# Attention with a relative-position bias and a mixture of adapters: two stages through DRAM rewritten as one hand-ordered pass over head pairs

## The chip, the cores and the metric

The kernel runs on one core of a Trainium2 chip. The metric is device time in microseconds (us) of one execution. A run is called slow when it is over 1.5% above the fastest of the same kernel. Engines: PE multiplies matrices and writes the results to a memory called PSUM (copying them out is called an eviction), ACT is ScalarE (exponentials and copies), DVE is VectorE (elementwise work), POOL is GpSimd (here it mostly issues loads that cast), SP issues other transfers.

## The reference, cut to what matters

There are 8 batches, 8 heads, 576 tokens and head dimension 64, all in float32. The attention has no mask. Its bias depends only on the distance of two tokens, through a table of 32 buckets per head; the last bucket holds for every distance of 128 or more.

```python
scores = q @ k.T / 8                      # per batch and head, 576 x 576
bias   = bias_table[bucket(|i - j|)]      # a Toeplitz matrix per head
x      = softmax(scores + bias) @ v       # -> 4608 tokens x 512
# experts: 8 adapters of rank 16; each token uses the two with the largest x @ w_gate
out    = x + sum over 2 experts of w_e * (x @ A[e]) @ B[e]
```

## The kernel before

It has two stages with DRAM between them, scheduled by a framework. Stage one goes head by head. Scores are held transposed (keys on partitions), so that the product with the values needs no transpose, and the bias is applied as a factor `exp(bias)` after the exponential:

```python
for jb in range(JB):                       # 5 blocks of keys (4 x 128 + 64)
    for n0, n1 in ((0, 512), (512, S)):
        nc.tensor.matmul(sc[:P, n0:n1], lhsT=kTs[:, jb*128:jb*128+P],   # 64 rows: one head
                         rhs=qTs[:, n0:n1], start=True, stop=True)
    nc.scalar.activation(e[:P, :], sc[:P, :], ACT.Exp, scale=scale)
    nc.vector.tensor_tensor(p[:P, :], e[:P, :], ebias[(h, jb)][:P, :], op=ALU.mult)
    for n0, n1 in ((0, 512), (512, S)):
        nc.tensor.matmul(pv[:, n0:n1], lhsT=v1[:P, jb, :],              # 64 + 1 columns
                         rhs=p[:P, n0:n1], start=(jb == 0), stop=(jb == JB - 1))
nc.vector.tensor_copy(o, pv[:D, :])         # then to DRAM as xT_d
nc.vector.tensor_copy(rsb, pv[D:D + 1, :])  # row sums, to DRAM as well
```

Ahead of it q, k and v are cast through DRAM to bf16, and 40 tiles `ebias` of 576 columns are built. Stage two reads x and the reciprocal sums back in 36 tiles of 128 tokens, and for each tile runs the gate (about ten small VectorE operations), the two expert matmuls, and four matmuls with an identity that add the residual.

The softmax here doesn't subtract the row's maximum and nothing guards it: scores larger than these inputs give would overflow.

## Time and profile before

The median was 625.53 us of three runs (622.73 to 628.53). These three lines are from the page of the kernel before: PE's busy time, then PE's busy share and its granted clock in 40 slices of the span, in tenths.

```profile
PE 453.0 (73%) x1960; PEld 181.3 (29%) x1960; DVE 326.4 (53%) x949; ACT 283.9 (46%) x537; POOL 193.1 (31%) x431
...
PE   0000895768899999999999999999999404555554
...
PEclk9999999999655555555555555555555556565556
```

The next lines are stretches of the span (from:to in us, length, then busy us and instruction count of PE, PE's weight loads, DVE, ACT and POOL, then the granted clock, as a share of full speed, the DMA share and GB/s).

```profile
core 0: us, PE busy (x) PEld busy (x) DVE busy (x) ACT busy (x) POOL busy (x), PEclk, DMA share, GB/s
62.00:150.00 88.00, 66.33 (x263) 24.73 (x264) 35.67 (x71) 53.62 (x89) 18.68 (x38) 1.00 0.77 189
200.00:450.00 250.00, 243.58 (x979) 91.25 (x978) 146.44 (x294) 134.37 (x216) 79.13 (x162) 0.50 0.36 79
520.00:600.00 80.00, 45.02 (x283) 26.70 (x282) 67.03 (x367) 31.35 (x115) 34.23 (x56) 0.56 0.89 234
```

From 200 to 450 us PE is busy for 243.58 of 250 us, at half clock, and no other engine comes near that: this stretch is bound by PE. After 520 us DVE leads.

The costliest groups of instructions (line, engine, operation, names, shapes, count | busy us, mean ns | idle time before them and what ended it). For a matmul, `64*128 64x512` says that the trace gives 64 active rows and 128 active columns for the weights, and 512 columns of the other operand; a "column" below is one of these 512, and "rows" are the 64.

```profile
L176 ACT ACTIVATE e<-sc 128x576 bf16<-128x576 f32 x256 | 161.8, 648 | 154.2 <-PE sc L171 116.9 <-PE pv L182 17.0 <-DVE p L179 9.8
L171 PE MATMUL sc<-pTq,pTk 64*128 64x512 bf16 x256 | 148.6, 595 | 15.4 <-ACT e L176 14.1 <-ACT pTk L149 0.7
L179 DVE TENSOR_TENSOR p<-e,ebias 128x576 bf16<-128x576 bf16 x256 | 105.2, 444 | 116.7 <-ACT e L176 98.7 <-ACT ebias L96 17.8
L171 PE MATMUL sc<-pTq,pTk 64*128 64x64 bf16 x256 | 63.2, 247 | 0.0
```

Two lines of PE's timeline (start us, us from the first start to the last end) show what the clock does. Both are 8 matmuls of the values, 4 x (512 + 64) columns:

```profile
145.78 2.13 PE L182 MATMUL pv<-p,v_914 128*65 128x512 bf16 x8
...
150.21 1.18 PE L182 MATMUL pv<-p,v_970 128*65 128x512 bf16 x8
```

The first took 2.13 us, the second 1.18. The clock record has only the values 0.5 and 1, and the second line lies in one of its few full stretches. **A trap:** the record begins at its first change, and the profile counts everything earlier as full. The 9s of the first ten slices are mostly wrong: until about 149 us the pace is that of half clock. Mean clocks of whole runs suffer from this too: 0.639 is listed for this trace, and 0.52 is left when the first 149.2 us are counted as half.

### The profile page before, as it was taken

The numbers are of one execution on the slowest core, as the hardware profiler recorded it, in microseconds if no ns is written. First come the engines' busy times: TensorE is split into PE (matmuls) and PEld (weight loads), VectorE is DVE, ScalarE is ACT, GpSimd is POOL, SyncE is SP. The second block draws the span as 40 slices with busy tenths as digits, with TensorE's granted clock in tenths as the row PEclk, the third lists the DMA queues.
The fourth block names the chain that finished last, engine by engine and source line by source line (L and its number), as shares of the span: only waits on it lengthen the run. The fifth ranks groups of instructions, "written<-read, shape, count | busy, mean of one in ns | idle before, by whom it ended". The sixth has DMA issues, their size and how long they took to land. (4 is left out here: it accounts for less than half of the span.)

```text
span 620.8 us, 7660 instructions
## 1 busy us (share of the span) xinstructions
PE 453.0 (73%) x1960; PEld 181.3 (29%) x1960; DVE 326.4 (53%) x949; ACT 283.9 (46%) x537; POOL 193.1 (31%) x431
## 2 busy tenths in 40 slices
PE   0000895768899999999999999999999404555554
PEld 0000331223333333333333333333333102333332
DVE  0000453237555656656565655656566417888884
ACT  0021674557554545555455555555555203333333
POOL 7040123114342423433232322323231055344420
PEclk9999999999655555555555555555555556565556
DMA  5999589669876775942222232101010089989872
GB/s 114 227 248 243 130 247 215 155 160 225 184 164 123 191 144 167 199 122 58 49 48 40 44 58 44 29 20 31 19 29 20 21 137 214 234 217 245 234 190 103
DMA packets 134388, 82.96 MB, mean 134 GB/s; under 512 B 110144, under 2 KB 115520, under 8 KB 134344
## 3 DMA queue, kind: packets, MB, share of 16 engines
q1 hardware_dynamic: 116168, 49.26, 31.2%
q0 software_dynamic: 13056, 28.48, 23.1%
q10 hardware_dynamic: 5120, 4.72, 2.4%
q8 instruction: 16, 0.26, 0.2%
q14 instruction: 28, 0.23, 0.1%
HBM read 67.93 MB, written 28.64 MB: 156 GB/s over the span
## 5 line engine op out<-in xcount | busy, mean ns | idle before, releaser
L176 ACT ACTIVATE e<-sc 128x576 bf16<-128x576 f32 (+1 forms) x320 | 201.0, 647 | 167.3 <-PE sc L171 126.1
L171 PE MATMUL sc<-pTq,pTk 64*128 64x512 bf16 (+3 forms) x640 | 209.9, 424 | 15.7 <-ACT e L176 14.3
L179 DVE TENSOR_TENSOR p<-e,ebias 128x576 bf16<-128x576 bf16 (+1 forms) x320 | 133.2, 445 | 142.5 <-ACT e L176 116.1
L171 PEld LDWEIGHTS <-pTk 64*128 64x128 bf16 (+1 forms) x640 | 56.5, 118 | 136.6 <-issue 132.8
L188 DVE CAST o<-pv 64x576 bf16<-64x576 f32 x64 | 48.0, 749 | 71.3 <-PE sc L171 58.3
L238 POOL DMA_DIRECT2D dv<-recips_d x72 | 44.1, 617 | 57.2 <-DVE lm L258 15.5
L143 PE MATMUL tpk<-ident,ntk 128*128 128x128 bf16 (+1 forms) x160 | 29.1, 284 | 38.9 <-DMA ntk<-k_bf 38.8
L96 ACT ACTIVATE ebias<-eb_tmp 128x576 bf16<-128x576 f32 (+1 forms) x40 | 26.7, 680 | 62.7 <-DMA eb_tmp<-gext_d 62.7
L192 DVE COPY rsb<-pv 1x576 f32<-1x576 f32 x64 | 48.1, 752 | 2.0
L143 PE MATMUL tpq<-ident,ntq 128*128 128x128 bf16 (+1 forms) x160 | 26.6, 287 | 24.2 <-DMA ntq<-q_bf 23.8
L193 POOL DMA_DIRECT2D sums_d<-rsb x64 | 32.4, 506 | 23.6 <-DVE rsb L192 23.6
L286 PE MATMUL ztT_ps<-ident,zt 128*128 128x128 bf16 x36 | 10.3, 287 | 40.2 <-DVE zt L281 37.4
L248 PE MATMUL zl<-AW,xTt 128*128 128x136 bf16 x144 | 22.4, 308 | 22.7 <-DMA dv<-recips_d 22.7
L244 DVE TENSOR_TENSOR xTt<-xTr,dv 128x512 bf16<-128x512 bf16 x36 | 24.9, 692 | 23.3 <-DMA xTr<-xT_d 13.7
L147 DVE COPY pTq<-tpq 128x576 bf16<-128x576 bf16 x32 | 14.6, 458 | 35.7 <-PE tpq L143 34.9
L297 ACT COPY ot<-dl 128x512 f32<-128x512 f32 x36 | 21.1, 586 | 27.0 <-PE dl L293 18.2
L143 PEld LDWEIGHTS <-ntk 128*128 128x128 bf16 (+1 forms) x160 | 13.9, 117 | 60.5 <-DMA ntk<-k_bf 39.8
L143 PEld LDWEIGHTS <-ntq 128*128 128x128 bf16 (+1 forms) x160 | 14.8, 127 | 39.7 <-issue 27.9
L290 PE MATMUL dl<-Bc,ztT 128*128 128x512 bf16 x36 | 21.0, 584 | 6.9 <-ACT ztT L288 6.6
L149 ACT COPY pTk<-tpk 128x576 bf16<-128x576 bf16 x32 | 20.0, 625 | 12.1 <-PE tpk L143 12.1
L248 PEld LDWEIGHTS <-xTt 128*128 128x128 bf16 x144 | 15.6, 138 | 23.3 <-issue 23.1
L293 PE MATMUL dl<-ident,xTt 128*128 128x128 bf16 x144 | 21.7, 302 | 0.0
(773 smaller groups left out, 519.7 us busy)
## 6 DMA issues: line engine op xcount, KB each, us to landing
eb_tmp<-gext_d SPq DMA_DIRECT2D x32, 288.0 KB, 4.0
dv<-recips_d POOLq DMA_DIRECT2D x72, 128.0 KB, 4.9
out_dram<-ot SPq DMA_DIRECT2D x36, 256.0 KB, 3.4
cb<-in_q_dram POOLq DMA_DIRECT2D x8, 576.0 KB, 6.1
q_bf<-cb SPq DMA_DIRECT2D x8, 576.0 KB, 3.7
cb<-in_k_dram POOLq DMA_DIRECT2D x8, 576.0 KB, 7.6
cb<-in_v_dram POOLq DMA_DIRECT2D x8, 576.0 KB, 8.0
k_bf<-cb SPq DMA_DIRECT2D x8, 576.0 KB, 4.5
```

The costliest lines, as they stand in the source:

```text
L96: nc.scalar.activation(eb[:P, :], trev, ACT.Exp)
L143: nc.tensor.transpose(tp[:, jb * 128:jb * 128 + P], nt[:P, jb, :], ident[:P, :P])
L171: nc.tensor.matmul(sc[:P, n0:n1], lhsT=kTs[:, jb * 128:jb * 128 + P], rhs=qTs[:, n0:n1], start=True, stop=True)
L176: nc.scalar.activation(e[:P, :], sc[:P, :], ACT.Exp, scale=scale)
L179: nc.vector.tensor_tensor(p[:P, :], e[:P, :], ebias[(h, jb)][:P, :], op=ALU.mult)
L188: nc.vector.tensor_copy(o, pv[:D, :])
L192: nc.vector.tensor_copy(rsb, pv[D:D + 1, :])
L193: nc.gpsimd.dma_start(out=sums_d.ap()[h, b * S:(b + 1) * S], in_=rsb)
L238: nc.gpsimd.dma_start(out=dv[hs * 64:(hs + 1) * 64, :, :], in_=bass.AP(tensor=rd.tensor, offset=rd.offset + hs * N + n0, ap=[[0, 64], [2 * ...
L244: nc.vector.tensor_tensor(xTt, xTr, dv, op=ALU.mult)
L248: nc.tensor.matmul(zl, lhsT=xTt[:, c, :], rhs=AW[:, c, :], start=(c == 0), stop=(c == 3))
L293: nc.tensor.matmul(dl[:, c * 128:(c + 1) * 128], lhsT=xTt[:, c, :], rhs=ident, start=False, stop=(c == 3), skip_group_check=True)
```

## The change

Its intent is to leave DRAM out between the stages, to do less per score, and to keep all engines busy at once. The order of instructions is set by hand. Per head pair:

```diff
+ # loads cast from f32 in the DMA (256-byte rows), token-major; PE transposes two heads at once
- nc.tensor.matmul(sc[:P, n0:n1], lhsT=kTs[:, jb*128:jb*128+P], rhs=qTs[:, n0:n1], ...)  # head by head
+ nc.tensor.matmul(sc[:, 1024:1152], lhsT=t[:, 0, g*128:(g+1)*128],      # tail queries, both heads
+                  rhs=tt[:, hp, 1, :], start=True, stop=True)
+ for h in range(2):                                                     # two heads = rows 0-63, 64-127 of t
+     s = slice(h * D, (h + 1) * D)
+     nc.tensor.matmul(sc[:, h*512:(h+1)*512], lhsT=t[s, 0, g*128:(g+1)*128],
+                      rhs=t[s, 1, :], start=True, stop=True)
- nc.vector.tensor_tensor(p[:P, :], e[:P, :], ebias[(h, jb)][:P, :], op=ALU.mult)
+ nc.vector.tensor_tensor(pm[:, :, q0:q1], pm[:, :, q0:q1],              # only the band |i-j| < 128+
+                         Mh[:, :, x0:x0 + q1 - q0], op=ALU.mult)
- nc.tensor.matmul(pv[:, n0:n1], lhsT=v1[:P, jb, :], rhs=p[:P, n0:n1], ...)   # x transposed
+ nc.tensor.matmul(acc[:, qb, h, :], lhsT=p[:, o:o + 128],               # x token-major:
+                  rhs=vn[:, g, 2*hp + h, :], ...)                        # weights = probabilities
... x stays in SBUF, normalised on eviction; gates for 512 tokens at once; residual added by VectorE
+ for i in range(NPAIR + 1):               # pair i's scores, pair i-1's values,
+     for g in range(5):                   # and one piece of the experts of an earlier batch
+         sc = qk(i, g); softmax_exp(i, g, sc)
+         if g == 0: transposes(i + 1)
+         if g == 1: norm_main(i - 1, pv_main(i - 1))
+         if g == 2: norm_rest(i - 1, pv_rest(i - 1))
+         if g in (0, 3, 4) and queue: queue.pop(0)()
+         band(i, g)
+ for f in queue: f()                      # what is left of the last batch
```

The factor outside the band is that of the last bucket; it is the same for all keys of a head, so it is divided out (the table has that bucket subtracted). Two PSUM buffers are shared by all accumulators, and two hold scores.

## The prediction

> **What bounds it now.** The span is 620.8 us in three parts (40-slice table). Until about 62 us little but DMA and bias tables runs. Then attention to 480 us: in the table of stretches, 200 to 450 us has PE busy 97%, DVE 59%, ACT 54%, at a granted clock of 0.50. Then the expert stage, behind a DRAM round trip (PE nearly idle for 20 us around 500), DVE 83% busy on small operations.
>
> Attention is bound by PE at half clock. The timeline shows a 512-column matmul every 0.43 us and a 64-column one every 0.07, i.e. 0.83 ns a column; a head streams 10 x 576 columns for scores and values plus 576 for transposes, 5.3 of its 6.25 us. (Before 149 us the clock row's 9s mislead: same pace.)
>
> **What the change does.**
> - Removed: q, k, v, x and row sums through DRAM, the stage boundary, 40 bias exponentials, two 0.75 us evictions per head, gate chains per 128 rows (now 512), identity matmuls for the residual.
> - PE, per head pair: the two heads' 64-row score matmuls stand together[...]. The trace already shows two 64-row matmuls starting 1 ns apart (411.87 us), so 512 columns should serve both. Changing between 64- and 128-row matmuls cost about 0.12 us (spacing 0.19 for 0.07)[...]. Scores: 4 x (0.11 + 0.43 + 2 x 0.12) + 0.53 = 3.6 us. Values: 32 matmuls of 65 columns at 0.07 and 9 of 130 at 0.115: 3.3. Transposes 1.0. Expert share 2.0. Sum 9.9 us at half clock, about 6 at full, against 12.5 now.
> - ACT: four exponentials of 1152, one of 640; at 0.83 ns per element and 0.17 fixed (576 took 0.648), 5.3 us.
> - DVE: band products over at most 384 columns per head 2.4, bf16 evictions 0.7, tails 0.3, normalisation 1.5, expert share 2.1: 7.0 us, from 0.445 us per 576-column bf16 product and 0.75 per 576 f32 eviction.
> - DMA: about 110,000 casting packets of 256 bytes. At 25 to 35 ns each (estimate from the 18 ns of 256-byte and the 27 or more of 512-byte packets here) 170 to 240 us of 16 engines: under the span, but a risk.
>
> **Critical path.** All per-pair work overlaps, so the largest engine decides: PE at half clock.[...] I expect half clock with windows of full clock, 9.4 us a pair with stalls: 300 us. Start about 25 us (batch 0's loads on one queue), tail (last batch's expert pieces) about 15. **Predicted 340 us, 80% range 295 to 395.** Chances: faster by over 2% 0.98, within 0.01, slower 0.01.
>
> **Right or wrong would show as:** PE busy over 85% from 25 us to the end at a mean clock of 0.5 to 0.7; DVE 65 to 75%, ACT 50 to 55%; 65-column matmuls 0.07 us apart; paired score matmuls starting together; no gap at an expert stage.
>
> **What would make it wrong.** Full clock throughout: DVE bounds, 270 to 295 us. Weight loads not hidden behind 65-column matmuls (0.11, not 0.07): 375. Casting packets over 45 ns[...]: PE waits on DMA, 380 or more. In-order stalls on the two accumulator buffers.

Four passages that no trace or run of this case shows are cut from it where marked. 32 pairs of 9.4 us make 300, and with 25 and 15 it is 340. Its times per instruction come from the trace before: ScalarE copies of 512 and 128 columns take 586 and 269 ns there, which gives the 0.83 ns and 0.17 us; weight loads at L171 take 114 ns in the mean, the 0.11 of an unhidden one; 256-byte packets took 18 ns and 512-byte ones 27 at the median. The 45 ns, the shares of the expert pieces, tails and normalisation, and the times named for what would make it wrong are estimates.

## The result, and the profile after

The changed kernel took 259.88 us (median of 4, 258.02 to 260.25), the kernel before 626.71 beside it. The ratio is 0.417, 95% interval 0.4135 to 0.4205. Ratios here are those of the record, made from fast runs, and not quite the ratio of the medians. The prediction said 340, with 295 to 395: the direction was right, the time well outside the range.

The same lines of the page, with DVE's row added:

```profile
PE 189.7 (74%) x2576; PEld 120.1 (47%) x2576; DVE 205.9 (80%) x641; ACT 165.4 (64%) x174; POOL 117.3 (46%) x155
...
PE   0020698797878868897799778987898788888852
...
DVE  3200678999898888999979898989998889989972
...
PEclk9999999999999999999889999999999999999965
```

Stretches: the steady part, and the end (columns as before).

```profile
60.00:195.00 135.00, 114.04 (x1609) 73.24 (x1606) 122.16 (x371) 102.76 (x108) 65.86 (x81) 0.99 1.17 111
235.00:257.00 22.00, 13.21 (x158) 7.59 (x154) 15.42 (x50) 4.30 (x7) 0.00 (x0) 0.76 0.31 109
```

PE now has the full clock nearly everywhere and is busy for 114.04 of 135 us; DVE leads with 122.16. The record's first entry is at 38.3 us, so the 9s left of that are again half clock. The groups:

```profile
L262 PE MATMUL sc<-kqT 64*128 64x512 bf16 x256 | 51.8, 402 | 0.0
...
L250 DVE COPY kqT<-kqps 128x1024 bf16<-128x1024 bf16 x32 | 21.8, 683 | 3.5 <-PE kqps L247 3.4
L457 DVE TENSOR_TENSOR o<-dl,x 128x512 f32<-128x512 f32 x32 | 21.8, 683 | 1.6 <-DMA out_dram<-o 0.8 <-PE dl L455 0.6
L348 DVE TENSOR_TENSOR x<-pvA,rcA 128x384 bf16<-128x384 f32 x32 | 17.8, 557 | 1.1
```

The pace of PE, before and after 38.3 us: each line at L310 is 6 matmuls of 65 columns, the weights loaded anew for each; the line at L262 is a pair of 64-row score matmuls.

```profile
35.82 0.51 PE L310 MATMUL pvA<-vn_86,p_227 128*128 128x65 bf16 x6
36.14 0.52 PE L310 MATMUL pvA<-vn_86,p_248 128*128 128x65 bf16 x6
36.47 0.52 PE L310 MATMUL pvA<-vn_86,p_255 128*128 128x65 bf16 x6
36.80 0.52 PE L310 MATMUL pvA<-vn_86,p_262 128*128 128x65 bf16 x6
...
37.68 0.61 PE L262 MATMUL sc<-kqT 64*128 64x512 bf16 x2
...
42.02 0.36 PE L310 MATMUL pvA<-vn_86,p_282 128*128 128x65 bf16 x6
42.22 0.35 PE L310 MATMUL pvA<-vn_86,p_301 128*128 128x65 bf16 x6
42.40 0.34 PE L310 MATMUL pvA<-vn_86,p_340 128*128 128x65 bf16 x6
42.59 0.35 PE L310 MATMUL pvA<-vn_86,p_367 128*128 128x65 bf16 x6
```

From start to start six of them take 0.33 us at half clock and 0.18 to 0.20 at full: 0.054 and about 0.031 us each, close to the columns alone (65 x 0.83 ns = 0.054, and half of it, 0.027, at full clock). So the 128-column weight loads are hidden, which was an open risk. The two score matmuls together took 0.61 us at half clock, where a single one took 0.595 in the mean in the kernel before.

The longest waits (who waited for whom, us in total, times, longest):

```profile
POOL vn_87 L69 <- PE pvB L336: 28.4, 3, 10.7
POOL vn_86 L69 <- PE pvB L336: 27.6, 3, 11.1
...
POOL kn L69 <- PE kqps L247: 18.2, 5, 4.6
...
ACT ex L412 <- DVE df L409: 17.0, 12, 5.2
DVE tlT_184 L239 <- POOL tlT_184 L221: 15.3, 1, 15.3
```

POOL waits for buffers to come free, not the other engines for loads: the casting packets (256 bytes of f32; the trace lists them as 128) took 32 ns at the median, inside the predicted 25 to 35, but they overlap. In the densest 4 us the 16 engines started 72 packets per us each on average, one per 14 ns. So loads were no limit after the start. The last line is a flaw at the start, tested below.

Pair by pair (from one eviction of transposed keys and queries, `kqT`, to the next) the time varies between 5.1 and 8.4 us, 6.7 in the mean, with the number of expert pieces in the pair.

### The profile page after: what moved, and what is told of

The parts are those of the page before. It is cut to its first block, busy times and chain, and to the rows that moved or that the text cites. A ratio compares the mean times of both kernels' runs of the same rounds, so it can differ in the third digit from the quotient of the medians.

```text
span 257.7 us, 6522 instructions
## 1 busy us (share of the span) xinstructions
PE 189.7 (74%) x2576; PEld 120.1 (47%) x2576; DVE 205.9 (80%) x641; ACT 165.4 (64%) x174; POOL 117.3 (46%) x155
## 4 chain that ended last, share of the span: by engine, by line
DVE 50%; PE 26%; ACT 7%; POOL 6%; issue 5%; DMA 3%; ACTq 0%; POOLq 0%; DVEq 0%
PE pvA L310 11%; DVE x L348 6%; PE sc L262 5%; DVE x L360 3%; DVE kqT L250 3%; DMA vn_86<-in_v_dram 3%; DVE o L457 3%; DVE xT L377 3%; PE pvA L304 2%; PE kqps L247 2%; DVE rcA L347 2%; POOL qn L69 2%; DVE rmB L358 2%; PE sc L258 1%; PE dl L455 1%
## 5 line engine op out<-in xcount | busy, mean ns | idle before, releaser
L262 PE MATMUL sc<-kqT 64*128 64x512 bf16 x256 | 51.8, 402 | 0.0
L69 POOL DMA_DIRECT2D kn<-in_k_dram x36 | 31.2, 896 | 19.1 <-PE kqps L247 18.2
L69 POOL DMA_DIRECT2D qn<-in_q_dram x36 | 31.0, 906 | 1.6 <-DMA vn_86<-in_v_dram 1.5
L258 PE MATMUL sc<-tlT_184,kqT 128*128 128x128 bf16 x64 | 14.5, 226 | 18.3 <-DVE kqT L250 13.0
L69 POOL DMA_DIRECT2D vn_87<-in_v_dram x16 | 14.0, 894 | 28.4 <-PE pvB L336 28.4
L69 POOL DMA_DIRECT2D vn_86<-in_v_dram x16 | 14.0, 896 | 27.7 <-PE pvB L336 27.6
L262 PEld LDWEIGHTS <-kqT 64*128 64x128 bf16 x256 | 12.4, 93 | 26.5 <-issue 17.4
L250 DVE COPY kqT<-kqps 128x1024 bf16<-128x1024 bf16 x32 | 21.8, 683 | 3.5 <-PE kqps L247 3.4
L457 DVE TENSOR_TENSOR o<-dl,x 128x512 f32<-128x512 f32 x32 | 21.8, 683 | 1.6 <-DMA out_dram<-o 0.8
L348 DVE TENSOR_TENSOR x<-pvA,rcA 128x384 bf16<-128x384 f32 x32 | 17.8, 557 | 1.1
L455 PE MATMUL dl<-Bb,zT 128*128 128x512 bf16 x32 | 13.3, 421 | 6.8 <-DVE zT L449 2.8
L258 PE MATMUL sc<-tlT_186,kqT 128*128 128x128 bf16 x64 | 14.2, 222 | 1.7 <-ACT p_571 L275 0.7
L360 DVE TENSOR_TENSOR x<-pvB,rmB 128x256 bf16<-128x256 f32 x32 | 13.6, 424 | 1.1
```

Source lines behind the costliest of these rows:

```text
L69: nc.gpsimd.dma_start(out=o, in_=src[b, h0:h1, j * 128:(j + 1) * 128, :] .rearrange("h p d -> p h d"))
L250: nc.vector.tensor_copy(t, ps)
L258: nc.tensor.matmul(sc[:, 1024:1152], lhsT=t[:, 0, g * 128:(g + 1) * 128], rhs=tt[:, hp, 1, :], start=True, stop=True)
L262: nc.tensor.matmul(sc[:, h * 512:(h + 1) * 512], lhsT=t[s, 0, g * 128:(g + 1) * 128], rhs=t[s, 1, :], start=True, stop=True)
L348: nc.vector.tensor_tensor(x[:, 0:3, 2 * hp:2 * hp + 2, :], acc[:, :, :, :D], rc.unsqueeze(3).to_broadcast((128, 3, 2, D)), op=ALU.mult)
L360: nc.vector.tensor_tensor(x[:, 3:5, 2 * hp:2 * hp + 2, :], acc[:, :, :, :D], rm.unsqueeze(3).to_broadcast((128, 2, 2, D)), op=ALU.mult)
```

## The clock beside the work: a count over the traces

In the traces, stretches between two changes of the clock are whole multiples of 3.413 us (in the kernel before 10.24, 361.81, 30.72 and 13.65 us, which are 3, 106, 9 and 4 of them; in the changed kernel 88.75 and 116.05, 26 and 34), so I cut every trace into windows of this length and counted the matmul columns started in each; windows before the record's first entry count as half clock. Doing so weighted by the share of the array's 128 rows that the matmul uses gives, over the traces of the two kernels and the twelve experiments:

```
clock now   row-weighted columns in the window   next window full / windows
half        under 2800                             1 / 514
half        2800 to 3199                          20 / 104
half        3200 and more                         53 /  53
full        under 2800                             0 /  61
full        2800 to 3199                          18 /  27
full        3200 to 3599                          29 /  33
full        3600 and more                        617 / 617
```

The traces of the two kernels alone give, in the same order, 0 of 160, 3 of 25 and 4 of 4 at half clock, and 0 of 6, 1 of 1, 2 of 3 and 57 of 57 at full.

Unweighted columns sort badly: of the half-clock windows with 3600 to 3999 columns only 4 of 36 are followed by full clock, and of those with 4000 or more 41 of 51. (4096 columns of 0.83 ns fill a window. No half-clock window of the kernel before has over 4032; the changed kernel, with scores side by side, has two, of 4642 and 4254.) In the kernel before four half-clock windows of 4032 columns had only 2592 or 2912 row-weighted ones, and the next stayed at half after each. The band of 2800 to 3200 is fuzzy, and a little above it too: in the changed kernel one full-clock window with 3712 columns (3200 row-weighted, at 123.7 us) was followed by half clock, and another with the same counts of columns (at 198.7 us) by full. Some matmul records are missing and ends are not recorded. Steady attention in the kernel before (200 to 450 us) has about 2440 row-weighted columns per window (1984 to 3136 in single windows), because over half of its columns use 64 rows. The weight of one half was checked against others: with the best single dividing line for each, over the half-clock windows, 64-row columns counted half leave 20 windows on the wrong side; counted 0, 0.25, 0.75 or 1 they leave 40, 24, 32 or 41. This is a correlation in the traces, found after the prediction, and the first experiments test it. What sets the clock on the chip, no trace shows.

## The experiments

All gave correct results. They ran later, and the changed kernel was not run again beside them. Their times are compared with its 259.88 us all the same: pairs that an edit does not touch take the same time in the traces (6.11 us for one such pair in the changed kernel, a_start, a_act and a_gate).

### b_sc128: 128 rows for the scores of the kernel before

```diff
- qTs = pair["q"][lo:hi, :]; kTs = pair["k"][lo:hi, :]
+ qTs = qz[hp % 4][hh]       # this head's queries in its 64 rows, zeros in the other 64
+ kTs = pair["k"]            # both heads' keys
```

> The kernel before, with one change: the score matmuls contract over 128 rows (both heads' keys as weights, the other head's queries zero) in place of 64; columns, count of matmuls and result are the same, no 64-row mode is left in them. Theory A[...]: granted clock goes from 0.64 to over 0.9, time to 480 to 540 us. Theory B (only how densely PE streams counts, whatever the rows): clock stays at 0.50 in attention, time 590 to 630 us. Theory C (used COLUMNS of the array count): as B.

Theory A, here and in the runs below, takes the count as a forecast: windows of many row-weighted columns are followed by full clock. Its 3000 is an estimate from the count, the middle of the band of 2800 to 3200.

It took 519.25 us against 618.43, ratio 0.8385 (0.8313 to 0.8457). PE and the clock in 40 slices, then three stretches:

```profile
PE   0100179356597679597799999999860055556544
...
PEclk9999995855589979699699999999995555555665
```

```profile
60.00:150.00 90.00, 58.52 (x263) 26.44 (x264) 38.66 (x78) 53.32 (x89) 18.69 (x38) 0.66 0.78 192
150.00:250.00 100.00, 79.98 (x514) 40.75 (x513) 77.83 (x163) 66.21 (x109) 43.62 (x89) 0.90 0.88 189
250.00:350.00 100.00, 92.09 (x621) 48.73 (x620) 92.97 (x197) 84.95 (x139) 49.27 (x103) 0.97 0.39 86
```

From 250 to 350 us the clock is 0.97, where the kernel before had 0.50, and DVE is now busiest with PE close behind. The first stretch is thin on work (it waits for loads) and stays mostly at half, the experts at the end too; so the mean is 0.80 and not over 0.9 as expected (0.73, against 0.52 for the kernel before, when the time ahead of the first record is counted as half). The extra rows hold zeros in the queries: the clock went from 0.50 to 0.97 with no data added.

### b_pv128: 128 array columns for the values of the kernel before

```diff
- v1 = qkp.tile([128, JB, D + 1], ...);  pv = pvp.tile([D + 1, S], ...)
+ v1 = qkp.tile([128, JB, 128], ...);    pv = pvp.tile([128, S], ...)    # extra columns of ones
```

> The kernel before, with one change: the value weights are 128 columns wide in place of 65 (the added ones give sums that nobody reads); rows and moving columns are the same. Theory A (rows count): clock stays near 0.64 in the mean and 0.50 in attention, time within 3% of before. Theory B (density alone): the same. Theory C (array columns or used area count): clock over 0.9 and time under 550 us.

It took 606.29 us, ratio 0.9806 (0.9721 to 0.9891), called unclear. The clock in 40 slices:

```profile
PEclk9999999999655558555555555855555555555555
```

It is half in nearly all of attention. Theory C falls: going from 65 to 128 columns of the array did not lift it. A few more full windows appear than before, worth 2%; whether the added columns had a part in it or PE's spacing moved windows near the band of 2800 to 3200 stays open.

### b_sc128m: rows or mode changes?

b_sc128 also took away every change between 64-row and 128-row matmuls. This run puts the changes back and keeps most of the rows.

```diff
- lhsT=kTs[:, ...], rhs=qTs[:, n0:n1]                       # (b_sc128: always 128 rows)
+ lhsT=(kTs if n0 == 0 else kTs[lo:hi])[:, ...],            # the 64-column part: 64 rows
+ rhs=(qTs if n0 == 0 else qTs[lo:hi])[:, n0:n1]
```

> As b_sc128 (the kernel before with 128-row scores), but the 64-column score matmul of each block goes back to 64 rows. The changes between 64- and 128-row mode are back in every block, while eight ninths of the score columns keep 128 rows. Theory A[...]: clock stays well above the 0.64 of before, 0.75 to 0.80, time 520 to 550 us. Rival (the mode changes[...] kept the clock low, and b_sc128 helped by taking them away): clock falls back to 0.64 to 0.67, time 590 to 620 us.

(Theory A as above. What a mode change does is not shown, only what it took in the kernel before: 0.19 us from start to start in place of 0.07.)

It took 530.73 us, ratio 0.8606 (0.8536 to 0.8676). Stretches:

```profile
60.00:150.00 90.00, 64.84 (x258) 25.84 (x258) 37.17 (x75) 51.90 (x86) 17.70 (x36) 0.63 0.75 188
150.00:250.00 100.00, 87.07 (x495) 40.00 (x494) 75.77 (x156) 65.42 (x107) 42.66 (x86) 0.89 0.83 180
250.00:350.00 100.00, 96.87 (x585) 45.55 (x584) 88.91 (x187) 79.70 (x130) 46.51 (x98) 0.95 0.43 93
```

The clock stays up at 0.95 from 250 to 350 us, with most of the rows in and the changes back. The run is 11.5 us longer than b_sc128; that is the mode changes together with a slightly lower clock (0.63, 0.89 and 0.95 in place of 0.66, 0.90 and 0.97), which were not separated.

### a_split: the changed kernel without score matmuls side by side

```diff
+ for h in range(2):
+     if h == 1: nc.tensor.matmul(sc[:, 1024:1152], ...)    # 128-row tail between the heads
      nc.tensor.matmul(sc[:, h*512:(h+1)*512], lhsT=t[s, ...], rhs=t[s, 1, :], ...)
```

> The changed kernel, with the 128-row tail matmul put between the two heads' 64-row score matmuls, so that they cannot run side by side. At full clock this adds about 0.2 us and two mode changes per group, about 1 us per pair: 275 to 300 us if the clock stays full (theory B, density alone, since PE gets denser). Theory A (rows times columns per window): at half clock a pair then takes about 11.8 us and gives 2700 row-weighted columns per window, under the 3000, so stretches at half clock should appear and last: mean clock 0.5 to 0.85, time 300 to 420 us.

It took 309.42 to 325.98 us in four runs, median 321.83; three are called slow beside the fastest. Their clock history differs, so there is no ratio. The trace kept is of one of the slow ones (318.15 us). Two groups of the same 24 value matmuls in its PE timeline, at 70 and at 202 us:

```profile
70.44 1.50 PE L312 MATMUL pvA<-vn,p 128*128 128x65 bf16 x24
```

```profile
202.09 0.91 PE L312 MATMUL pvA<-vn,p 128*128 128x65 bf16 x24
```

The first 1.50 us and then 0.91: this kernel runs at half clock until about 90 us (and again for 20 us), although PE is busy for 38.52 us between 60 and 100. In that time its pairs take 10 to 11.8 us; later, at full clock, 6.8 to 9.1. From 38 to 90 us its windows have 2640 row-weighted columns in the mean, where the count has 1 of 514 (under 2800) followed by full clock. That the slower pairs are themselves what keeps the windows so thin is the author's reading, not shown. Stretches at half clock that last are what theory A expected; the listed mean of 0.951 hides it, for the reason given above. Fast run against fast run, side-by-side scores are worth 50 us of 260. That is above the 15 to 40 of theory B, so some of it should be the clock, but the fast run's own clock history was not kept.

### a_start: the start

```diff
- nc.gpsimd.memset(vt ...); nc.gpsimd.memset(vn ...); nc.gpsimd.memset(t, 0.0)   # POOL, t = tlT
+ nc.vector.memset(...)                                                            # all three on DVE
- load_v(0); load_kq(0, 2, H)
+ load_kq(0, 2, H); load_v(0)
```

> The changed kernel, with the memsets of the constant tiles moved from POOL to DVE and batch 0's remaining keys and queries loaded before its values. If the 13 us before the first scores are the POOL queue (tlT's memset stands behind 14 load issues), the first scores start near 15 us, those of pair 1 near 21, and the whole is 7 to 11 us shorter, about 250 us. If the transfers themselves bound the start, the gain is under 3 us. The steady part (about 6.6 us a pair) stays.

It took 253.53 us, ratio to the kernel before 0.4098 (0.4069 to 0.4128), where the changed kernel had 0.417 (0.4135 to 0.4205). This is the fastest kernel. The copy that makes the first `kqT` started at 14.5 us in place of 27.0, but the second came 9.6 us after it in place of 2.6: going by the trace, the POOL queue was about one half of the delay, and the transfers of the six heads behind it the other (in the chain that ended last, a load of queries takes 9.0 us there). The edit's two parts, memsets and load order, were not separated. The gain of 6.4 us is a little under the 7 to 11 expected.

### a_fullband: the bias over all columns

```diff
- nc.vector.tensor_tensor(pm[:, :, q0:q1], pm[:, :, q0:q1], Mh[:, :, x0:x0 + q1 - q0], op=ALU.mult)
+ nc.vector.tensor_tensor(pm, pm, MF[:, 2*hp:2*hp+2, 384 - g*128:896 - g*128], op=ALU.mult)
```

> The changed kernel, with the bias product over all columns instead of the band (factors of 1 outside it; same count of instructions). It adds about 0.95 us of VectorE work per pair, 30 us in all. VectorE bounds: about 285 to 290 us. If another engine or the loads bound: under 272.

It took 288.84 us, 29 more than the changed kernel. The clock row of its page:

```profile
PEclk9999999599959999999799989999799799999975
```

The number looks like VectorE's alone, but the clock has a part in it: between its first record at 38.0 us and 276.9 us this run has six half-clock stretches, 27 us in all, where the changed kernel has one of 3.41 us. Five pairs in a row (85 to 120 us in the changed kernel) are at full clock in both traces. There VectorE's busy time grew by 0.95 us a pair and the pair's time by 0.65 (0.54 to 0.74); two pairs that fell into a half-clock stretch grew by 1.8 and 2.0. So the added VectorE work cost about two thirds of its length in these five pairs; that the rest of the 29 us comes with the clock is an estimate from the two slowed ones. The band is worth 29 us with both.

### a_act: evictions moved from VectorE to ScalarE

```diff
- nc.vector.tensor_copy(xT[:, :, half*256:(half+1)*256], ps);  nc.vector.tensor_copy(zT, ps)
+ nc.scalar.copy(xT[:, :, half*256:(half+1)*256], ps);         nc.scalar.copy(zT, ps)
```

> The changed kernel, with two evictions of the expert stage (xT and zT, 14.3 us of VectorE in the profile) moved to ScalarE (about 21 us there). If VectorE's total work bounds the steady part (206 us busy in 258), 8 to 13 us shorter, about 248 us. If the in-order chain PE to ScalarE bounds it, no gain or slower (258 to 265), as ScalarE's queue then waits for PE's transposes between two exponentials.

It took 267.66 us (266.72 to 268.02): 7.8 us longer, a little beyond the 258 to 265 of the rival, which is right here. VectorE's busy time fell from 205.9 to 195.4 us, ScalarE's rose from 165.4 to 183.8, and pairs with expert pieces went from at most 8.4 to 9.2 us. ScalarE stood 7.8 us in all in front of these copies, waiting for PE's transposes (xT 3.7, zT 4.1). So the sum of VectorE's work is not the bound either: the copies stand between the exponentials that feed everything else. The clock has little part in it: two half-clock windows in place of one, and the 9.2 us are found in pairs without one.

### a_unfused: experts after the last pair

```diff
- if g in (0, 3, 4) and i > 0 and queue: queue.pop(0)()      # (x gets 8 buffers)
```

> The changed kernel, with all pieces of the expert stage run after the last pair instead of between the pairs. VectorE-bound theory: its 206 us stay, but beside the pairs only some 140 of them are left, so ScalarE (5.2 us a pair) bounds the pairs at 5.5 to 5.8 us, 28 + 180 us, and the experts then take 60 to 80 us alone: 270 to 290 us. If the loads bound the pairs (rival), the pairs get no faster than 6.6 us and the total is 310 or more. With less work on PE the clock should show more half-clock windows in the expert part, as its profile in the kernel before did (0.5 to 0.6).

It took 304.70 us, 45 more. Stretches: pairs alone, then experts alone.

```profile
60.00:195.00 135.00, 110.33 (x1592) 70.68 (x1587) 112.76 (x317) 125.04 (x125) 65.44 (x80) 1.00 1.07 69
200.00:300.00 100.00, 71.11 (x590) 44.71 (x588) 69.14 (x215) 5.84 (x16) 0.00 (x0) 0.56 0.26 93
```

Pairs alone take 5.4 us in the mean (5.1 to 5.2, and 6.2 for one in four), nearly all of it ScalarE's five exponentials (it is busy for 125.04 of 135 us), and not the loads, which now keep up with faster pairs. The experts alone take 100 us, with PE sparse and at 0.56. That is longer than the 60 to 80 expected.

### a_gate, a_best, a_combo, a_combo_pool: trying for more

a_gate cuts the gate of the experts in three so that its small exponential is queued later. a_best joins a_start's memsets, a_act, and loads of the first two pairs per head. a_combo joins a_start's memsets and a_gate with such loads, ahead of the values. a_combo_pool moves one bias product to POOL. (The loads of a_best and a_combo are left out of the cut.)

```diff
  m_gate(...): ... df = lg - max
- nc.scalar.activation(ex, df, ACT.Exp); ... gate = ...       # all in one piece
+ (a later piece) nc.scalar.activation(ex, df, ACT.Exp)       # a_gate, a_combo, a_combo_pool
+ (the piece after) mk, sm, gate, and the z matmuls
- nc.vector.tensor_tensor(pm[...], pm[...], Mh[...])           # g == 0, three pairs of four
+ nc.gpsimd.tensor_tensor(pm[...], pm[...], Mh[...])           # a_combo_pool
```

> The changed kernel, with the gate of the expert stage cut in three pieces, so that its small exponential enters ScalarE's queue one slot after VectorE's part (in the changed kernel ScalarE stood 17.0 us in front of 12 such exponentials, of which about 6 us at the end after the last pair). If that queueing costs time in the pairs, 4 to 9 us shorter: 251 to 256 us. If VectorE's sum alone bounds, no change within 2 us, since its work is the same.

> The changed kernel with a_start's memsets, with a_act's two evictions, and with batch 0's first two pairs loaded per head (4 issues of 512 rows in place of 8 of 256) before its values, the other heads after them. Start 8 to 11 us shorter than in the changed kernel, steady part about 0.3 us a pair shorter: 238 to 244 us.

> a_start's memsets, a_gate's pieces, and batch 0's loads as in a_best but with its remaining keys and queries before its values; without a_act. Start: first scores near 11 us, pair 2 near 22, values of pair 0 near 26, so 9 to 12 us shorter than the changed kernel, and a_gate's gain on top: 240 to 247 us.

> a_combo, with the first of the five bias products of a pair (0.42 us of VectorE) on POOL, for three pairs of four from batch 1 on: 21 products, 9 us less on VectorE. If VectorE's sum bounds: 5 to 9 us shorter than a_combo. If it bounds only in some pairs, or POOL's products come late behind load issues[...]: no gain or slower.

None became faster than a_start, and three missed what was expected: a_gate 266.77 us (266.24 to 267.89), a_best 261.34, a_combo 260.22 (255.03 to 261.25, three of four called slow). a_combo_pool took 263.95, its "no gain or slower". The clock row of a_gate's page:

```profile
PEclk9999999999999997999599988999899979997985
```

Where the changed kernel's record has one half-clock window of 3.41 us between 38.3 and 246.5 us, a_gate's has six half-clock stretches, starting at 99.4, 126.7, 157.5, 184.8, 212.1 and 239.4 us: in the new order of pieces one place in each batch leaves PE thin for a window (2048 to 3072 row-weighted columns), and the next runs at half clock. Some pairs took 8.6 us and were followed by others of 7 to 8. The wait that a_gate was made to remove did shrink (its exponentials waited 6.5 us in all for the end piece in place of 17.0), but it was not the one that mattered. How much of the 6.9 us is clock and how much order was not separated. In a_combo_pool the product on POOL is slow:

```profile
L299 POOL TENSOR_TENSOR p<-p,M 128x512 bf16<-128x512 bf16 x21 | 24.7, 1174 | 88.3 <-ACT p L284 88.3
```

1174 ns against 0.41 us on DVE.

## Why the prediction was wrong

- **"PE at half clock … I expect half clock with windows of full clock" is the step that failed.** From 38.3 us on the record shows full clock but for one window and the tail. The prediction took half clock as given by the kernel before, where it held at 97% busy. With 128 rows for the scores it rose there from 0.50 (200 to 450 us) to 0.97 (250 to 350 us, b_sc128), and to 0.95 with the mode changes back (b_sc128m). The change runs the two heads' 64-row scores side by side (0.61 us for two at half clock) and has 128 rows elsewhere; a_split, which keeps the two heads apart in time, brings stretches of half clock back in its trace. At 9.9 us a pair, its own half-clock estimate, the count would already have pointed to full clock: about 9700 row-weighted columns a pair (60 to 195 us) give 3340 per window, and all 53 half-clock windows of 3200 and more were followed by full clock. In place of 9.4 us a pair "with stalls" the runs show 6.7, which is 86 us over 32 pairs; the forecast missed by 80. Its signs failed with it: PE 74% busy (over 85 expected), DVE 80% (65 to 75), ACT 64% (50 to 55). The clue was in the trace before: a window of the expert stage with 3392 columns of 128 rows (83% of 4096) was followed by full clock, while attention had the same 3394 columns in the mean and stayed at half. "97% busy" was no gapless PE either (3394 of the 4096 columns that fill a window at 0.83 ns).
- The branch named for this case, "Full clock throughout: DVE bounds, 270 to 295 us", came nearest, still 10 us high. "7.0 us" of VectorE per pair was right as a sum of durations (6.9), but VectorE was busy for 6.0 (171.57 us in 190, at 6.68 us a pair): instructions in a row overlap, as VectorE's timeline shows:

```profile
191.09 0.55 DVE L289 TENSOR_TENSOR p_3351<-p_3351,M 128x768 bf16<-128x768 bf16 x1
191.55 0.68 DVE L377 COPY xT<-xps 128x1024 bf16<-128x1024 bf16 x1
192.15 0.41 DVE L289 TENSOR_TENSOR p_3378<-p_3378,M 128x512 bf16<-128x512 bf16 x1
192.49 0.21 DVE L293 TENSOR_TENSOR p_3378<-p_3378,M 128x128 bf16<-128x128 bf16 x1
192.62 0.68 DVE L377 COPY xT<-xps 128x1024 bf16<-128x1024 bf16 x1
193.22 0.28 DVE L282 TENSOR_TENSOR p_3396<-p_3396,MH 128x256 bf16<-128x256 bf16 x1
```

  The first lasts 0.55 us and the next starts 0.46 later; 0.68 is followed after 0.60. At some 19 instructions a pair this is the 0.9 us that a sum of durations counts twice. DVE alone does not set the time either: pairs without expert pieces run at ScalarE's 5.1 to 5.3 us, the heavy ones at 7 to 8.4.
- "65 columns at 0.07": 0.054 at half clock. Too high, and the rival of unhidden loads (0.11) is excluded.
- Right: ScalarE 5.3 us (5.4 a pair where it bounds, a_unfused); paired scores (started 3 to 4 ns apart, 0.61 us for two, and a_split); band products 2.4 us (their durations sum to 2.4 a pair); about 25 us of start (first scores at 27.8) and 15 of tail (the last values end near 240.5 us, the span at 257.7).
- The "in-order stalls" that it named are part of what is left: where ScalarE has a piece of the experts in front of scores (a_act). How much they cost the changed kernel is open: a_gate took one such wait out and gained nothing.
- Not shown: how the 367 us divide between DRAM left out, less work and the clock. No run takes the parts apart, but for the side-by-side scores, the band and the order of the experts.

## What to carry to other kernels

A busy PE at half clock is a question, not a fact to carry into a prediction: here all 53 half-clock windows of 3.41 us with 3200 and more columns, weighted by the rows in use, were followed by full clock, and 1 of 514 under 2800; 128-row scores, the added 64 rows filled with zeros, saved 16% of the kernel before (b_sc128). Whether other kernels show the same is not shown: count their windows. Before trusting a clock row, check the pace of equal matmuls in the timeline, above all left of the first record. Here VectorE was busy for 205.9 us, PE for 189.7 and ScalarE for 165.4, and moving 10.5 us off VectorE made the kernel 7.8 us longer (a_act); test such a move, and look at the clock after it.
